# Transposing the decays of a linear attention without a clamp, and storing the first FFN's sums from another queue

## The chip, the cores and the metric

The kernel runs on one core of a Trainium2 chip. The metric is the device time of one execution in microseconds (us). A core has five engines with instruction streams of their own: PE (matrix products and transposes), DVE (vector), ACT (activations), POOL (GpSimd) and SP, which here only issues transfers. An engine runs its own instructions in order and waits on semaphores for the others. Transfers are issued from a queue of an engine, here SP's and, before the change, ACT's.

## The reference

A linear attention with decays is followed by two feed-forward networks (FFN) over the same 3072 tokens. There are B = 4 batches, H = 8 heads, S = 768 tokens and D = 48 features of a head:

```python
for t in range(S):
    cur = einsum('bhd,bhe->bhde', u[None] * k[t], v[t])
    y[t] = einsum('bhd,bhde->bhe', r[t], state + cur)
    state = w[t][..., None] * state + einsum('bhd,bhe->bhde', k[t], v[t])
x = y, as 3072 tokens of 384
h = x @ w_in;  x = (h * clip(h + 3, 0, 6) / 6) @ w_out             # 384 -> 2048 -> 384
h = x @ w_in2; s = h * softmax(h); x = (layernorm(s) * g) @ w_out2 # 384 -> 1024 -> 384
```

The decays w are drawn between 0.80 and 0.95. Everything is float32.

## The kernel before

The attention runs in chunks of 128 tokens. A tile is one chunk of one batch: 24 tiles, tile i being chunk g = i // 4 of batch b = i % 4. Four tiles make a group of 512 tokens, the width of a matrix product in the first FFN. Each tile passes five stages. `stw` checks that the decays lie in the range of the fast path (two activations on ACT that write `junk` and add up what lies outside) and clamps them; a kernel whose checks fire takes a general path. `st0` transposes w and r (`wt`, `rt`) and runs prefix products of the decays on DVE (`q` backwards, `e` forwards). `st1` transposes k and multiplies it into q, while POOL forms r * k * u (written over r) whose sums are `d`. `st2` makes `ktp`/`ktok`, the keys with tokens on the partitions, and the scores (`pa`), whose diagonal `am` POOL builds from d and DVE overwrites below the diagonal. `st3` adds the chunk to the state (`s_st`, over `sp`, the decayed state from POOL) and forms the output `yt`, which ACT and DVE split into a high part `xh` and a low part `xl`.

For tiles 0 to 9 the clamp writes a copy `wc`, which PE transposes: on DVE for tiles 0 to 3, on POOL for tiles 4 to 9. The tiles from 10 on (`LATE`) hold w, r and k in another layout (`late_w`, `late_r`, `late_k`), clamp `late_w` in place on POOL, and DVE transposes them (`flip`).

The first FFN runs in 96 slots n, 16 for each group of 512 tokens. `ffn_in(n)` is nine matmuls of 128x512 into a PSUM sum `h` (two buffers), ACT makes `t`, DVE finishes it, ACT rounds it to `gh`, and POOL or DVE forms the rest `gl`. `ffn_out` follows two slots later with nine matmuls into the three sums `y`. At the last of a group's 16, ACT scales the three sums into `ye` (L751) and its queue stores them to DRAM as `y1d` (L752). `ye` and `xl` rotate through the same two buffers. The weights of the first FFN come as packed words: during the first 16 slots SP loads a piece (`raw`, three buffers), and ACT and DVE decode it (`dec`, L50, L53, L66, then `w_h` on ACT and `w_l`, L72, on DVE).

Phase 2 is the second FFN over 24 tiles of 128 tokens, each read back from `y1d` by `load_y`. It starts after the 96 slots and the two that follow.

The order: for the first four tiles SP and POOL run in the order of the code; after that SP does, and DVE too from slot 78 (`NA`) on. All other engines are ordered by a scheduler when the program is built, which can therefore move any of their instructions when one is taken out. In a slot the loads of a late tile (`load_late`, the last of them `vt`) stand ahead of `ffn_out`, and so ahead of the stores.

Of the kernel before, what the change touches and what calls it, by code (L numbers as in the profile page):

```python
# [8 lines left out]
F32 = mybir.dt.float32  # L9
# [4 lines left out]
ALU = mybir.AluOpType  # L14
# [4 lines left out]
P = 128  # L19
W_LO, W_HI = 0.75, 1.25  # L20
# [258 lines left out]
def fast_path(  # L279
# [14 lines left out]
    nc = tc.nc  # L294
    B, H, S, D = r.shape
# [12 lines left out]
    NSLOT = NG * M1  # L308
# [7 lines left out]
    y1d = dram.tile([NG, P, KD, GT], F32, name="y1d")  # L316
# [25 lines left out]
        out=causal.bitcast(F32), in_=ones, pattern=[[1, P]], compare_op=ALU.is_gt, fill=0.0, base=0,  # L342
# [5 lines left out]
    atp = right.enter_context(tc.tile_pool(name="atp", bufs=2, side="right"))  # L348
# [28 lines left out]
    def w1_b(m):  # L377
        split(nc, dec_b(nc, *wst.pop(m)), w1_h[:, m, :], w1_l[:, m, :], nc.vector)
# [81 lines left out]
    def flip(nm):  # L460

        t = ps_tile(nm + "t")
        nc.vector.transpose(
            out=t.rearrange("p h (b j) -> p h j b", j=4),
            in_=late[nm].rearrange("p h (j d) -> p h j d", d=D)[:, :, :, 0:32],
        )
        return t
# [13 lines left out]
    def ps_in(i, nm, spare):  # L481
        if i >= B:
            return ps_tile(nm)
        return ps_y.tile([P, GT], F32, tag=spare, name=nm).rearrange("p (h t) -> p h t", t=P)

    def trans(dst, src):
        s2 = src.rearrange("p h d -> p (h d)")
        for hp in range(HP):
            nc.tensor.transpose(out=dst[0:DP, hp, :], in_=s2[:, hp * P:hp * P + DP], identity=ident)

    def stw(i):
        a = at[i]
        if i >= LATE:
            x = late["w"][:, :, 0:4 * D - 16]
            junk = atp.tile([P, HP, 4 * D - 16], mybir.dt.uint8, tag="junk", name="junk", bufs=1)
            nc.scalar.activation(
                out=junk, in_=x, func=ACTF.Relu, scale=-1.0, bias=b_lo, accum_out=chk[:, 3 * i:3 * i + 1]
            )
            nc.scalar.activation(
                out=junk, in_=x, func=ACTF.Relu, bias=b_hi, accum_out=chk[:, 3 * i + 1:3 * i + 2]  # L500
            )
            nc.gpsimd.tensor_scalar(out=x, in0=x, scalar1=W_HI, scalar2=W_LO, op0=ALU.min, op1=ALU.max)
            return
        wc = atp.tile([P, H, 64], F32, tag="wc", name="wc", bufs=1)
        flat = slice(0, H * 64 - 16)
        eng = nc.vector if i < B else nc.gpsimd
        eng.tensor_scalar(
            out=wc.rearrange("p h d -> p (h d)")[:, flat], in0=a["w"].rearrange("p h d -> p (h d)")[:, flat],
            scalar1=W_HI, scalar2=W_LO, op0=ALU.min, op1=ALU.max,
        )  # L510
        a["wc"] = wc
        junk = atp.tile([P, H, D], BF16, tag="junk", name="junk", bufs=1)
        nc.scalar.activation(
            out=junk, in_=a["w"][:, :, 0:D], func=ACTF.Relu, scale=-1.0, bias=b_lo, accum_out=chk[:, 3 * i:3 * i + 1]
        )
        nc.scalar.activation(
            out=junk, in_=a["w"][:, :, 0:D], func=ACTF.Relu, bias=b_hi, accum_out=chk[:, 3 * i + 1:3 * i + 2]
        )

    def st0(i):  # L520
        a = at[i]
        g = i // B
        if i < LATE:
            wt = ps_in(i, "wt", "y0")
            trans(wt, a["wc"])
            rt = ps_in(i, "rt", "y1")
            trans(rt, a["r"])
        else:
            wt, rt = flip("w"), flip("r")
        q = atp.tile([P, HP, C + 1], F32, tag="q", name="q")  # L530
        e = atp.tile([P, HP, C], F32, tag="e", name="e")
        nc.gpsimd.memset(q[0:DP, :, C:C + 1], 1.0)
        for hp in range(HP):
            nc.vector.tensor_tensor_scan(
                out=q[0:DP, hp, 0:C][:, ::-1], data0=wt[0:DP, hp, :][:, ::-1], data1=ones[0:DP, :],
                initial=1.0, op0=ALU.mult, op1=ALU.mult,
            )
        nc.vector.reciprocal(out=e[0:DP, :, 0], in_=q[0:DP, :, 0])
        for hp in range(HP):
            nc.vector.tensor_tensor_scan(  # L540
                out=e[0:DP, hp, 1:C], data0=wt[0:DP, hp, 0:C - 1], data1=ones[0:DP, 0:C - 1],
                initial=e[0:DP, hp, 0:1], op0=ALU.mult, op1=ALU.mult,
            )
        nc.vector.tensor_tensor(out=e[0:DP], in0=rt[0:DP], in1=e[0:DP], op=ALU.mult)
        a.update(q=q, e=e)
# [152 lines left out]
    def st3(i):  # L698
# [3 lines left out]
        out_x(i)  # L702

    stages = [stw, st0, st1, st2, st3]


# [29 lines left out]
    def ffn_out(n):  # L736
        g, m = divmod(n, M1)
        if m == 0:
            y_ps[g] = [ps_y.tile([P, GT], F32, tag=f"y{c}", name=f"y{c}") for c in range(KD)]
        gh, gl, _ = g_t.pop(n)  # L740
        for c in range(KD):
            cs = slice((KD + c) * P, (KD + c + 1) * P)
            wh, wl = w1_h[:, m, cs], w1_l[:, m, cs]
            for j, (a, b) in enumerate([(wh, gh), (wh, gl), (wl, gh)]):
                nc.tensor.matmul(  # L745
                    out=y_ps[g][c], lhsT=a, rhs=b, start=(m == 0 and j == 0), stop=(m == M1 - 1 and j == 2)
                )
        if m == M1 - 1:
            ye = xp.tile([P, KD, GT], F32, tag="xl", name="ye")
            for c in range(KD):  # L750
                nc.scalar.activation(out=ye[:, c, :], in_=y_ps[g][c], func=ACTF.Copy, scale=1.0 / 6.0)  # L751
                nc.scalar.dma_start(out=y1d[g, :, c, :], in_=ye[:, c, :])  # L752
            del y_ps[g]

    def range_in(ws):
# [42 lines left out]
    def w2_load(j):  # L798
        if j < M2:
            src = w_in2[:, 2 * j * P:2 * (j + 1) * P].rearrange("(k p) f -> p k f", p=P)  # L800
        else:
            src = w_out2[(j - M2) * P:(j - M2 + 1) * P, :].unsqueeze(1)
        wst[j] = [load_dec(nc, w2["dec"], src, bufs=3)]
# [17 lines left out]
    def load_y(i):  # L821
        g, b = divmod(i, B)
        t = w2["y"].tile([P, KD, C], F32, tag="y1", name="y1")
        nc.sync.dma_start(out=t, in_=y1d[g, :, :, b * C:(b + 1) * C])
        yh = w2["y"].tile([P, KD, C], F32R, tag="yh", name="yh")
        yl = w2["y"].tile([P, KD, C], F32R, tag="yl", name="yl")
        nc.gpsimd.tensor_scalar(out=yh, in0=t, scalar1=1.0, scalar2=1.0, op0=ALU.mult, op1=ALU.mult)
        nc.gpsimd.tensor_tensor(out=yl, in0=t, in1=yh.bitcast(F32), op=ALU.subtract)
        yt[i] = (yh, yl)
# [4 lines left out]
    def load_to(n):  # L834
        while nxt[0] < min(n, LATE):
            load_in(nxt[0])
            load_v(nxt[0])
            nxt[0] += 1
# [43 lines left out]
    for n in range(NSLOT + LAG):  # L882
        if n < NSLOT:
            ffn_in(n)
        if n == 4 * (JOIN - B) - 2:
            ps_late()
        for i, s in sorted(sched.get(n, []), key=lambda x: (x[0] - 2 * (x[0] >= JOIN and x[1] == 3), x[1])):
            stages[s](i)
            if s == NS - 1 and JOIN <= i + 1 < NTILE:
                state_in(i + 1)  # L890
            if s == 3:
                load_to(i + 3)
            if s == (0 if i + 1 == LATE else 2) and LATE <= i + 1 < NTILE:
                load_late(i + 1)
        if n >= LAG:
            ffn_out(n - LAG)
        if n + LD < M1:
            w1_b(n + LD)
        if n + LD + 1 < M1:
            w1_a(n + LD + 1)  # L900
        if n + LD + 3 < M1:
            w1_load(n + LD + 3)
        if n == M1:
            dec_st.close()
            late_open()
        if n == M1 + 1:
            late_mask("diag", ident)
        if n == M1 + 2:
            late_mask("mask", causal)
        if n == NA:  # L910
            row = range_a()
            right.close()
            w2_open()
            for j in range(3):
                w2_load(j)
            order.close()
            order = ctx.enter_context(ExitStack())
            order.enter_context(tc.manual_schedule(engines={mybir.EngineType.SP, mybir.EngineType.DVE}))
        j = n - NA
        if 1 <= j <= 2 * M2:  # L920
            w2_b(j - 1)
            if j + 2 < 2 * M2:
                w2_load(j + 2)
        if NA < n < NSLOT:
            ffn_low(n)
        if 0 <= j < 2 * M2:
            w2_a(j)
    load_y(0)
    load_y(1)
    order.close()  # L930


# [110 lines left out]
```

## Time and profile before

| | before |
|---|---|
| median of 3 runs | 775.6 us (774.93 to 776.07) |
| the profiled execution's own time | 774.71 us |
| its span, first to last instruction | 772.6 us |
| busy: PE, DVE, ACT, POOL | 733.3, 535.1, 333.1, 266.3 us |
| mean granted clock of PE | 0.971 |

A row of the trace's timeline gives the start, the duration, the engine, the line, the operation, the tiles (output <- inputs), and in brackets how long the engine had been idle and what ended that. "SPq" and "ACTq" are the sequencers that issue transfers. Where several instructions of a kind follow each other, the row gives their number and joint time. "PE rt <- issue" means that PE's transposes of r started after idle time that the trace puts down to nothing else.

### The profile page before, as it was taken

How to read it: one execution, taken by the hardware profiler on the slowest of the kernel's cores; microseconds unless marked ns; L12 is line 12 of the kernel's file. 1: busy time of each engine (PE TensorE's matmuls, PEld its weight loads, DVE VectorE, ACT ScalarE, POOL GpSimd, SP SyncE). 2: the span in 40 equal slices, each digit the busy share in tenths (PEclk: the TensorE clock that was granted, in tenths of full speed). 3: DMA queues.
4: the chain of work that ended last, by engine and by line, in shares of the span. 5: the costliest groups of instructions: out<-in, count | busy, mean ns of one | idle time of the engine just before them, and what ended most of it. 6: DMA issues, size and time to landing. Idle time of an engine off the chain costs nothing. (4 is left out here: it accounts for less than half of the span.)

```text
span 772.6 us, 14109 instructions
## 1 busy us (share of the span) xinstructions
PE 733.3 (95%) x5308; PEld 620.9 (80%) x5308; DVE 535.1 (69%) x1012; ACT 333.1 (43%) x647; POOL 266.3 (34%) x397
## 2 busy tenths in 40 slices
PE   5778797999999999999999999999999999999996
PEld 4556685888887888878888888888899999999995
DVE  6979889658777777777787865787555555555552
ACT  3455456334434333433334334654444444444442
POOL 5556547742332333333333311224322222222200
PEclk9669998999999999999999999999999999999998
DMA  9794754534344344443335203422111111111001
GB/s 168 172 172 124 178 133 101 108 86 97 86 95 121 86 104 87 93 117 82 91 74 130 63 1 103 144 94 70 65 48 44 41 42 48 45 42 42 31 22 36
DMA packets 151405, 67.31 MB, mean 87 GB/s; under 512 B 101792, under 2 KB 145952, under 8 KB 151328
## 3 DMA queue, kind: packets, MB, share of 16 engines
q1 hardware_dynamic: 148736, 61.60, 33.6%
q10 hardware_dynamic: 2592, 4.72, 1.6%
q8 instruction: 44, 0.72, 0.4%
q14 instruction: 33, 0.27, 0.1%
HBM read 56.33 MB, written 9.44 MB: 85 GB/s over the span
## 5 line engine op out<-in xcount | busy, mean ns | idle before, releaser
L745 PE MATMUL y<-gh,w_h 128*128 128x512 f32 x288 | 115.8, 402 | 0.0
L720 PE MATMUL h<-xh,w_h 128*128 128x512 f32 x288 | 113.4, 394 | 0.0
L720 PE MATMUL h<-xl,w_h 128*128 128x512 f32 x288 | 113.1, 393 | 0.0
L745 PE MATMUL y<-gl,w_h 128*128 128x512 f32 x288 | 113.1, 393 | 0.0
L745 PE MATMUL y<-gh,w_l 128*128 128x512 f32 x288 | 113.0, 392 | 0.0
L720 PE MATMUL h<-xh,w_l 128*128 128x512 f32 x288 | 112.7, 391 | 0.0
L726 ACT ACTIVATE gh<-t 128x512 fp32r<-128x512 f32 x96 | 60.4, 629 | 116.4 <-DVE t L725 116.4
L724 ACT ACTIVATE t<-h,cols 128x512 f32<-128x512 f32 x96 | 65.2, 680 | 93.2 <-PE h L720 91.2
L725 DVE SCALAR_TENSOR_TENSOR t<-t,h 128x512 f32<-128x512 f32 x96 | 65.1, 678 | 34.6 <-ACT t L724 34.3
L734 DVE TENSOR_TENSOR gl<-t,gh 128x512 fp32r<-128x512 f32 x80 | 66.7, 834 | 24.1 <-ACT gh L726 19.1
L78 DVE TENSOR_REDUCE nm<-h 128x1 f32<-128x1024 f32 x24 | 29.4, 1225 | 61.5 <-PE h L950 61.4
L977 PE MATMUL po<-w_oh,qh 128*128 128x384 f32 x192 | 67.2, 350 | 0.3 <-ACT qh L966 0.3
L745 PEld LDWEIGHTS y<-gh,w_h 128*128 128x128 f32 x288 | 54.3, 189 | 13.9 <-issue 3.2
L977 PE MATMUL po<-w_oh,ql 128*128 128x384 f32 x192 | 64.8, 337 | 0.1
L977 PE MATMUL po<-w_ol,qh 128*128 128x384 f32 x192 | 64.8, 338 | 0.0
L745 PEld LDWEIGHTS y<-gh,w_l 128*128 128x128 f32 x288 | 54.5, 189 | 11.8
L720 PEld LDWEIGHTS h<-xh,w_h 128*128 128x128 f32 x288 | 54.6, 190 | 11.5
L720 PEld LDWEIGHTS h<-xh,w_l 128*128 128x128 f32 x288 | 54.6, 190 | 11.4
L720 PEld LDWEIGHTS h<-xl,w_h 128*128 128x128 f32 x288 | 54.6, 190 | 11.3
L745 PEld LDWEIGHTS y<-gl,w_h 128*128 128x128 f32 x288 | 54.6, 190 | 10.4
L966 ACT ACTIVATE qh<-pt 128x512 fp32r<-128x512 f32 x48 | 26.1, 595 | 78.4 <-PE pt L964 78.4
L950 PE MATMUL h<-w_ih,yl 128*128 128x512 f32 x144 | 56.4, 392 | 0.0
(132 smaller groups left out, 1482.6 us busy)
## 6 DMA issues: line engine op xcount, KB each, us to landing
raw<-in_moe_w_out_dram SPq DMA_DIRECT2D x24, 384.0 KB, 6.2
raw<-in_moe_w_in_dram SPq DMA_DIRECT2D x48, 128.0 KB
r<-in_r_dram SPq DMA_DIRECT2D x24, 192.0 KB, 3.0
k<-in_k_dram SPq DMA_DIRECT2D x24, 192.0 KB, 4.2
y1d<-ye ACTq DMA_DIRECT2D x18, 256.0 KB, 3.2
y<-y1d SPq DMA_DIRECT2D x24, 192.0 KB, 2.7
out_dram<-os SPq DMA_DIRECT2D x24, 192.0 KB, 1.9
v<-in_v_dram SPq DMA_DIRECT2D x20, 192.0 KB, 4.7
```

Source lines behind the costliest of these rows:

```text
L78: nc.vector.tensor_reduce(out=nm, in_=h, axis=AX.X, op=ALU.max, negate=True)
L720: nc.tensor.matmul(out=h, lhsT=a, rhs=b, start=(j == 0), stop=(j == len(ops) - 1))
L724: nc.scalar.activation(out=t, in_=h, func=ACTF.Relu, bias=three)
L725: nc.vector.scalar_tensor_tensor(out=t, in0=t, scalar=6.0, in1=h, op0=ALU.min, op1=ALU.mult)
L726: nc.scalar.activation(out=gh, in_=t, func=ACTF.Copy)
L734: eng.tensor_tensor(out=gl, in0=t, in1=gh.bitcast(F32), op=ALU.subtract)
L745: nc.tensor.matmul(out=y_ps[g][c], lhsT=a, rhs=b, start=(m == 0 and j == 0), stop=(m == M1 - 1 and j == 2))
L950: nc.tensor.matmul(out=h[:, fs], lhsT=a[:, c, :], rhs=b_[:, c, fs], start=(j == 0), stop=(j == len(ops) - 1))
L966: nc.scalar.activation(out=qh[:, ms, :], in_=pt, func=ACTF.Copy)
L977: nc.tensor.matmul(out=po, lhsT=x[:, m, :], rhs=y[:, m, :], start=(n == 0), stop=(n == 3 * M2 - 1))
```

## The change

Three things. The clamp is gone from both layouts, and PE transposes the loaded w itself; the two checks on ACT and the general path stay. The stores of `ye` are issued by SP. The first two `load_y` stand in slot 94, ahead of the last group's stores, and no longer after the loop.

```diff
@@ stw
-            nc.gpsimd.tensor_scalar(out=x, in0=x, scalar1=W_HI, scalar2=W_LO, op0=ALU.min, op1=ALU.max)
             return
-        wc = atp.tile([P, H, 64], F32, tag="wc", name="wc", bufs=1)
-        flat = slice(0, H * 64 - 16)
-        eng = nc.vector if i < B else nc.gpsimd
-        eng.tensor_scalar(
-            out=wc.rearrange("p h d -> p (h d)")[:, flat], in0=a["w"].rearrange("p h d -> p (h d)")[:, flat],
-            scalar1=W_HI, scalar2=W_LO, op0=ALU.min, op1=ALU.max,
-        )
-        a["wc"] = wc
@@ st0
-            trans(wt, a["wc"])
+            trans(wt, a["w"])
@@ ffn_out
                 nc.scalar.activation(out=ye[:, c, :], in_=y_ps[g][c], func=ACTF.Copy, scale=1.0 / 6.0)
-                nc.scalar.dma_start(out=y1d[g, :, c, :], in_=ye[:, c, :])
+                nc.sync.dma_start(out=y1d[g, :, c, :], in_=ye[:, c, :])
@@ main loop
+        if n == NSLOT - 2:
+            load_y(0)
+            load_y(1)
         if NA < n < NSLOT:
             ffn_low(n)
         if 0 <= j < 2 * M2:
             w2_a(j)
-    load_y(0)
-    load_y(1)
```

The line numbers of the changed kernel are eight or nine lower from here on. What the change does to the order is seen at three places. The first is POOL around tile 3's diagonals (`am`) and tile 4's clamp. Before:

```order
L399 MEMSET w 128x8x16
L507 TENSOR_SCALAR wc<-w 128x496
L532 MEMSET q 112x4
L399 MEMSET r 128x8x16
L399 MEMSET k 128x8x16
L627 TENSOR_TENSOR am<-ident,d 128x512 x2
L399 MEMSET w 128x8x16
L507 TENSOR_SCALAR wc<-w 128x496
```

Now, the same stretch of POOL:

```order
L399 MEMSET w 128x8x16
L523 MEMSET q 112x4
L399 MEMSET r 128x8x16
L399 MEMSET k 128x8x16
L618 TENSOR_TENSOR am<-ident,d 128x512 x2
L399 MEMSET w 128x8x16
L551 TENSOR_TENSOR r<-r,k 128x8x48
```

No instruction that reads a loaded tile stands ahead of `am` any more. On ACT, too, the rounding `w_h` of weight piece 1 now stands ahead of the first check of tile 4, behind which it stood before.

The second is DVE at the end of tile 6 (its state sums, `s_st_117`) and the start of tile 7 (q from `wt`, later q times `kt`). Before:

```order
L53 SCALAR_TENSOR_TENSOR dec<-raw,dec 128x768
L649 TENSOR_TENSOR s_st_117<-kv,sp 48x4x48 x2
L66 TENSOR_SCALAR raw<-raw 128x768
L72 TENSOR_TENSOR w_l<-dec,w_h 128x768
L725 SCALAR_TENSOR_TENSOR t<-t,h 128x512
L691 TENSOR_TENSOR xl<-yt,xh 128x3x128
...
L544 TENSOR_TENSOR e<-rt,e 112x512
L725 SCALAR_TENSOR_TENSOR t<-t,h 128x512
L72 TENSOR_TENSOR w_l<-dec,w_h 128x768
L558 TENSOR_TENSOR q<-kt,q 112x4x128
```

Now:

```order
L53 SCALAR_TENSOR_TENSOR dec<-raw,dec 128x768
L716 SCALAR_TENSOR_TENSOR t<-t,h 128x512
L66 TENSOR_SCALAR raw<-raw 128x768
L72 TENSOR_TENSOR w_l<-dec,w_h 128x768
L640 TENSOR_TENSOR s_st_117<-kv,sp 48x4x48 x2
L682 TENSOR_TENSOR xl<-yt,xh 128x3x128
...
L535 TENSOR_TENSOR e<-rt,e 112x512
L716 SCALAR_TENSOR_TENSOR t<-t,h 128x512
L549 TENSOR_TENSOR q<-kt,q 112x4x128
L72 TENSOR_TENSOR w_l<-dec,w_h 128x768
```

The state sums moved behind t, L66 and w_l; the product q with `kt` moved ahead of w_l. On PE the transposes `rt` of tile 7 stand eight matmuls later than before.

The third is ACT at the end of the second group. Before:

```order
L751 ACTIVATE ye<-y_1882 128x512
L752 DMA y1d<-ye 128x512
L726 ACTIVATE gh<-t 128x512
L751 ACTIVATE ye<-y_1883 128x512
L751 ACTIVATE ye<-y_1884 128x512
L752 DMA y1d<-ye 128x512 x2
L724 ACTIVATE t<-h,cols 128x512
L589 ACTIVATE ktok<-ktp 128x448
```

Now:

```order
L742 ACTIVATE ye<-y_1862 128x512
L742 ACTIVATE ye<-y_1863 128x512
L717 ACTIVATE gh<-t 128x512
L742 ACTIVATE ye<-y_1864 128x512
L715 ACTIVATE t<-h,cols 128x512
L580 ACTIVATE ktok<-ktp 128x448
```

No store stands between the activations. On SP the three stores now stand in one piece behind the three `vt` loads, and ahead of the next tile's loads of `late_w`.

## Rows read from the trace of the kernel before

**Rows 1.** Windows: us, busy us of each engine (instructions), PEclk, DMA share, GB/s.
```profile
0.00:140.00 140.00, 109.73 (x889) 86.96 (x890) 119.33 (x210) 68.16 (x144) 80.80 (x109) 0.85 0.69 149
140.00:760.00 620.00, 617.90 (x4391) 529.14 (x4390) 414.47 (x801) 262.81 (x499) 185.45 (x288) 1.00 0.29 74
```

**Rows 2.** What PE waited for, whole span: us in total, times, longest us.
```profile
PE rt L489 <- issue: 7.6, 3, 4.6
PE ktp L587 <- DVE q L558: 5.5, 3, 4.1
...
PE yt L669 <- DVE am L630: 5.1, 2, 3.8
...
PE yt L662 <- ACT ktok L589: 2.0, 2, 1.1
```

**Rows 3.** The clamps' lines L507, L502: duration ns min/median/max, first and last start.
```profile
L507 POOL TENSOR_SCALAR wc<-w x6: 600/828/1191, 42.2 to 148.0; 128x496 f32<-128x496 f32 x6
L507 DVE TENSOR_SCALAR wc<-w x4: 479/604/1205, 4.1 to 24.5; 128x496 f32<-128x496 f32 x4
L502 POOL TENSOR_SCALAR late_w<-late_w x14: 773/775/777, 154.1 to 427.3; 128x704 f32<-128x704 f32 x14
```

**Rows 4.** Timeline around tile 3's diagonals and tile 4's clamp.
```profile
40.16 0.53 DVE L599 TENSOR_REDUCE d<-r 128x8 f32<-128x384 f32 x1
...
42.24 0.60 POOL L507 TENSOR_SCALAR wc<-w 128x496 f32<-128x496 f32 x1 [3.74 <-DMA w<-in_w_dram]
...
43.24 2.76 POOL L627 TENSOR_TENSOR am<-ident,d 128x512 f32<-128x512 f32 x2
...
43.66 1.44 DVE L72 TENSOR_TENSOR w_l<-dec,w_h 128x768 fp32r<-128x768 f32 x1 [2.09 <-ACT w_h L71]
```

**Rows 5.** Timeline: tile 4's d, the load behind it, and weight piece 6.
```profile
52.27 0.55 DVE L599 TENSOR_REDUCE d<-r 128x8 f32<-128x384 f32 x1 [1.37 <-POOL r L561]
...
53.00 3.29 SPq L400 DMA_DIRECT2D r<-in_r_dram  x1
...
68.56 0.91 ACT L63 ACTIVATE dec<-raw 128x768 f32<-128x768 f32 x1 [2.03 <-DMA raw<-in_moe_w_out_dram]
```

**Rows 6.** Timeline of DVE and PE at the end of tile 6 and in tile 7.
```profile
117.59 0.71 DVE L649 TENSOR_TENSOR s_st<-kv,sp 48x192 f32<-48x192 f32 x2
...
118.41 0.62 PE L489 MATMUL rt<-ident,r 128*112 128x128 f32 x4 [1.29 <-issue]
...
119.10 0.39 PE L745 MATMUL y<-gl,w_h 128*128 128x512 f32 x1
...
119.33 0.39 PE L745 MATMUL y<-gh,w_l 128*128 128x512 f32 x1
...
128.55 0.67 DVE L725 SCALAR_TENSOR_TENSOR t<-t,h 128x512 f32<-128x512 f32 x1
...
131.06 0.68 DVE L558 TENSOR_TENSOR q<-kt,q 112x512 f32<-112x512 f32 x1
```

**Rows 7.** Timeline: a subtract of POOL and a decoding step of DVE beside it.
```profile
88.88 1.99 POOL L734 TENSOR_TENSOR gl<-t,gh 128x512 fp32r<-128x512 f32 x1 [4.28 <-ACT gh L726]
...
89.66 2.03 DVE L53 SCALAR_TENSOR_TENSOR dec<-raw,dec 128x768 int32<-128x768 int32 x1
```

**Rows 8.** Timeline at the end of the second group: ACT's queue, SP and DVE.
```profile
248.47 1.03 ACTq L752 DMA_DIRECT2D y1d<-ye  x2
249.54 0.69 ACT L724 ACTIVATE t<-h,cols 128x512 f32<-128x512 f32 x1 [0.62 <-ACT ye L751]
...
252.38 1.67 SPq L437 DMA_DIRECT2D vt<-in_v_dram  x3
...
255.70 0.54 DVE L691 TENSOR_TENSOR xl<-yt,xh 128x384 fp32r<-128x384 f32 x1
```

**Rows 9.** The page's DMA issues: queue, count, KB each, median us to landing.
```profile
y1d<-ye ACTq DMA_DIRECT2D x18, 256.0 KB, 3.2
```

**Rows 10.** Timeline: the longest hold of DVE in one instruction after 140 us.
```profile
391.97 4.70 DVE L734 TENSOR_TENSOR gl<-t,gh 128x512 fp32r<-128x512 f32 x1 [0.30 <-ACT gh L726]
```

## The prediction

> **What bounds it now.** I read the windows first, then the waits of PE, then the timeline around each wait. The windows cut the run in two [rows 1]. From 140 to 760 us PE is busy 617.90 of 620 us, so nothing but fewer idle microseconds on PE can shorten that stretch, and there are about 2.1 of them. From 0 to 140 us PE is busy only 109.73 us, which leaves 30.3 us idle, while DVE is busy 119.33 of the 140. So in the front DVE, and what DVE waits for, sets the pace; PE waits behind it. The waits say the same by name [rows 2]: the long ones in the front end on DVE work (q, am), or on "issue" in front of rt, which is a place in PSUM that DVE gives back late. The 2.0 us on ktok, an ACT result, are the two gaps after 140 us. A saving counts if it shortens the front's DVE chain or removes one of those two gaps; anywhere else PE has other matmuls to run.
>
> **The clamps that go.** Four run on DVE (0.60, 0.48, 0.60, 1.21: 2.9 us), six on POOL for tiles 4 to 9 (0.60 to 1.19), fourteen on POOL for the late tiles (0.775 each) [rows 3]. The late fourteen are worth nothing: the view of that line lists nobody who waited for one of them, since the transpose behind each comes much later in DVE's order. I cost them at 0.
>
> **The four on DVE and the first one on POOL.** Taking 2.9 us out of DVE is not yet 2.9 us off the end: by hand through the new order I get about 1 us earlier at the scans of tile 2, 1.9 us after the 1.21 us clamp of tile 3, and then almost nothing, since the second and third pieces of the FFN weights were waited for as transfers there. What is left decides at 42 to 46 us [rows 4]. The clamp of tile 4 waited 3.74 us on POOL for the transfer of w, and the two diagonals of tile 3 (am) stood behind it, although their input d, started at 40.16, had been ready at 40.7. PE waited 3.8 us for that am [rows 2]. With the clamp gone POOL has nothing between: am can start at about 40.5 instead of 43.24. On ACT the rounding w_h of weight piece 1 now stands ahead of the range check of tile 4, which waits for the same transfer, so w_l need not wait its 2.09 us. The two together bring am, xl and the d of tile 4 forward by about 3.2 us (bounds: 2.1, the wait of w_l alone, to 3.8, the wait of PE).
>
> **What of that lasts.** Tile 4's d now ends 3.2 us earlier, and the r load of tile 6, which reuses the buffer that d reads, was issued right after it [rows 5]. But weight piece 6 is only issued behind tile 6's loads on SP, and ACT waited 2.03 us for it to land; DVE's own first step on that piece stands in its order just behind. The queue was slow there: one r load took 3.29 us to issue. If these transfers do not move, the whole 3.2 is given back at 69 us; if they move with d, it all stays. I take half, **-1.6** (bounds 0 and -3.2), because the load behind d moves, while the transfers ahead of it do not.
>
> **Tiles 6 and 7.** Before, the two state sums of tile 6 (s_st) ran at 117.59, right behind L53, and rt of tile 7 could then start, having waited 1.29 us [rows 6]. Now t, L66 and w_l stand ahead of s_st: 0.6 + 0.5 + 0.9, and 0.2 for gaps, is 2.2 us later. In exchange rt stands eight 512-column matmuls later on PE; at the 0.23 us from one start to the next [rows 6] that is 1.8 us of cover. Cost: **+0.4** (bounds 0 and +2.2). In tile 7 the product q*kt now stands ahead of w_l. Before it ran at 131.06 behind a w_l that waited for ACT; it can now follow t, which started at 128.55 and takes 0.6 to the next start, so at 129.15: **-1.9** out of the 4.1 us that PE waited for ktp [rows 2, 6] (bounds 0 and -1.9).
>
> **POOL out of DVE's way.** L53 took 2.03 us while POOL ran a subtract of 1.99 us from 88.88 [rows 7]; the DVE clamp that took 1.21 instead of 0.60 ran beside POOL work too. Six POOL clamps less could give DVE some of this back; I take 0 (bounds 0 and -1.0), since POOL moves its next subtract into the hole. The Trainium skill ("SBUF — State Buffer", section "SBUF: two separate sides") says that DVE and GpSimd share a pair of ports as an exclusive lock, held for a whole instruction, and that a DVE instruction with two SBUF inputs fully blocks against a GpSimd one that reads SBUF. The two rows agree with it: 2.03 is what L53 needs alone plus the rest of POOL's 1.99. By that rule each POOL clamp removed beside such an instruction would be a gain, and the sum would be lower by up to 1.0.
>
> **The stores moved to SP.** At the boundary of the second group ACT's queue gave 1.03 us to two stores, t came 0.62 us after the last ye, ktok after t, and PE waited 1.1 us for ktok [rows 2, 8]. Without stores ACT saves those 1.03 and the 0.3 of the first store, more than the 1.1. The third group has the same picture with 0.9: that is the 2.0 in two times of [rows 2]. I leave 0.2 for each: **-1.6** in all (bounds -2.0 and +2). On SP the three stores stand behind the vt loads of the same slot. Those were issued at 252.38 and took 1.67 us, so the stores go out from 254.1 and not from 247 to 249.5; with about 1 us for three issues and the 3.2 us to landing, which the page has for these stores [rows 9], the last lands near 258.3. The first xl of the next but one group takes that buffer, and it ran at 255.70: DVE may stand there for 2.6 us. I cost that at 0, because at 391.97 DVE was held for 4.70 us in one instruction [rows 10] in a stretch in which PE did not stop [rows 1]; without that cover it is 2.6 for each boundary. The Trainium skill ("DMA: Bandwidth & Descriptors", section "Issuing engines are not separate DMA queues") says that another issuing engine saves only the sequencer's time to start a transfer, usually small. Here that time is the 1.03 above, and by itself it would give about the same sum.
>
> **The first phase 2 loads.** PE goes from the last FFN matmul to the first of phase 2 without waiting on them, so their earlier place is worth 0. What hides them are the matmuls of the last slots, 18 a slot; without that cover a load would cost its issue and landing once, some 3 us, and the new place, ahead of three stores, is on the safe side of that.
>
> **Sum.** -1.6 + 0.4 - 1.9 + 0 - 1.6 = -4.7, say 770.0 against the profiled execution's own 774.7 (a span of 772.6 and 2.1 around it). The median of the runs, 775.6, lies 0.9 above that execution, so I forecast 770.9 against the median.
>
> **Rivals.**
> *More stays.* The transfers move with DVE: -3.2 at 46 us lasts, POOL's -1.0 is had, rt costs 0, the boundaries give 2.0: -8.1, or 767.5. For it: DVE has idle time enough in the front, 20.7 us of 140 [rows 1]. Against it: the 2.03 us wait for piece 6 [rows 5].
> *The front gives nothing.* Landings take back the 3.2, and PE's ktp waits for something else that is late, such as kt or the rounding on ACT: only the boundaries are left, -1.6, or 774.0. For it: in the front each engine waits in turn for the others, and POOL or ACT can be late next.
> *Slower: the stores hold xl.* At the four boundaries from the second to the fifth group DVE stands 2.6 us at xl, and behind it stand t of the running FFN slot and the scans. PE has two sums h in flight, and stops when both wait for t. If nothing covers it, this is +10.4, with -3.1 in the front and no gain at the boundaries: +7.3, or 782.9; with only half uncovered +2.1, or 777.7. It decides from the point where a hold of DVE is longer than PE's matmuls in hand; the 4.70 us hold speaks against it, but that one was in gl, not ahead of t.
> *It does not do what it says.* The stores on SP cost nothing, but ktok is still late for another reason (the three ye on ACT remain): the front alone, -3.1, or 772.5. It lies inside the range.
>
> **Chances.** Forecast 0.50, more stays 0.15, front gives nothing 0.17, ktok still late 0.07, slower 0.11. The range has to leave out the slower case and the far end of "more": from 766.5 to 775.5. A difference of 0.2%, 1.55 us, is about what a measurement of this kernel can tell from no change. Faster than 774.05: the forecast, more, ktok, and half of the nothing case, some of the forecast's mass lost to sizes I misjudge: 0.77. Within 0.2%: 0.12. Slower: 0.11.
>
> **What would show it.** Right: am of tile 3 starts before 41 us and PE's wait for am shrinks from 5.1 to about 1.5; tile 4's d starts near 49; ktp waits 2 to 3 us less; the ktok line is gone from PE's waits; PE is busy about 110 us in a front that ends 3 us earlier. Wrong: w_l or L50 of piece 6 waits longer on the raw transfer than the 2.03 on ACT (front gives nothing); rt of tile 7 waits over 3 us; xl waits on the y1d store with PE idle right behind (slower). The forecast also falls if PE's clock, 0.85 on average before 140 us [rows 1], a mean over stretches at either of its levels, falls further or less after the shorter stalls than it did.

## The result, and the profile after

The changed kernel takes 769.01 us in the median (767.82 to 770.91), the kernel before 775.7: a ratio of 0.9917, 95% interval 0.9904 to 0.9931. A second measurement, beside later runs, gave 768.86 and 0.9920 (0.9903 to 0.9937). The forecast was 770.9, within 766.5 to 775.5. The profiled execution took 769.93 us with a span of 768.2; that is 4.8 less than the profiled one of before, while the medians are 6.7 apart, since this one lies 0.9 above its median and that of before lay 1.0 below its own.

The windows of the changed kernel, which answer to [rows 1]:

```profile
0.00:140.00 140.00, 113.39 (x905) 87.80 (x906) 119.09 (x207) 68.32 (x145) 75.87 (x104) 0.88 0.69 149
140.00:760.00 620.00, 619.40 (x4397) 530.31 (x4397) 416.40 (x803) 263.75 (x501) 174.99 (x273) 1.00 0.30 75
```

PE is busy 3.7 us more in the first 140 us, and idle only 0.6 us in the 620 that follow. DVE is as busy in the front as it was (119.09 to 119.33): what it was spared in clamps it now does of later work. What PE waited for, as in [rows 2]:

```profile
PE rt L489 <- issue: 8.5, 3, 4.1
PE yt L660 <- DVE am L621: 7.8, 6, 2.8
PE wt L489 <- DMA w<-in_w_dram: 4.3, 1, 4.3
PE h L711 <- DVE w_l L72: 2.0, 1, 2.0
PE ktp L578 <- DVE q L549: 1.1, 2, 0.9
```

The ktok line is gone, ktp fell from 5.5 to 1.1; rt rose from 7.6 to 8.5 and am from 5.1 to 7.8. The profile of the second measurement has rt at 9.1 and am at 6.0.

One cut helps to read all the runs. The first `ye` of the first group marks the end of the front, the first `ye` of the last group the end of the five groups with boundaries between, and the rest is the last stores and phase 2. The marks are starts of ACT's rows in the timeline of one profiled execution of each kernel; the medians and ratios are those of the timed runs, each against the kernel before on the same chip.

| kernel | median us | ratio to before (95%) | first ye | to the last group's | rest |
|---|---|---|---|---|---|
| before | 775.7 | 1 | 162.65 | 379.85 | 230.10 |
| changed | 769.01 | 0.9917 (0.9904-0.9931) | 160.11 | 377.75 | 230.34 |
| changed, second measurement | 768.86 | 0.9920 (0.9903-0.9937) | 158.59 | 377.67 | 230.34 |
| before, stores on SP | 780.95 | 1.0076 (1.0059-1.0092) | 164.09 | 377.71 | 239.10 |
| before, loads moved | 775.17 | 1.0008 (0.9994-1.0021) | 164.01 | 379.92 | 230.07 |
| before, clamps out | 771.20 | 0.9959 (0.9943-0.9974) | 159.85 | 379.95 | 230.00 |
| changed, stores back on ACT | 771.88 | 0.9961 (0.9947-0.9976) | 159.18 | 379.87 | 230.05 |
| changed, loads back | 776.86 | 1.0018 (1.0006-1.0031) | 160.46 | 377.73 | 237.21 |
| changed, DVE's clamps back | 771.31 | 0.9953 (0.9934-0.9971) | 161.51 | 377.75 | 230.14 |
| changed, POOL's early clamps back | 771.20 | 0.9947 (0.9928-0.9966) | 161.70 | 377.84 | 230.26 |
| changed, late clamps back | 771.03 | 0.9953 (0.9934-0.9971) | 159.79 | 377.70 | 231.71 |
| changed, state sums first | 770.05 | 0.9939 (0.9925-0.9954) | 159.59 | 378.16 | 230.15 |
| changed, four w_l on POOL | 769.46 | 0.9940 (0.9923-0.9958) | 163.33 | 378.30 | 229.97 |
| changed, three buffers for q | 770.16 | 0.9933 (0.9917-0.9949) | 160.82 | 378.11 | 230.07 |

The middle column is the cleanest: 379.9 with the stores on ACT, 377.7 to 378.3 with them on SP, whatever else the kernel does. Between kernels that differ in the stores alone the move is worth 2.1 to 2.2 us there. The front has a spread of its own: the changed kernel itself ended it at 160.11 and at 158.59. The three kernels with all clamps end it at 162.65, 164.01 and 164.09, the five profiles without any clamp and with nothing else in the front altered between 158.59 and 160.46. The means, 163.6 and 159.6, lie 3.9 apart. One timed execution of the kernel with three buffers for q took 1036.63 us at a mean granted clock of 0.657; it is in that kernel's median and not in its ratio.

### The profile page after: what moved, and what is told of

It reads as the page before. It is cut to its first block, busy times and chain, and to the rows that moved or that the text cites. A ratio compares the mean times of both kernels' runs of the same rounds, so it can differ in the third digit from the quotient of the medians.

```text
span 768.2 us, 14066 instructions
## 1 busy us (share of the span) xinstructions
PE 734.3 (96%) x5308; PEld 619.3 (81%) x5308; DVE 535.5 (70%) x1008; ACT 332.6 (43%) x647; POOL 250.9 (33%) x377
## 5 line engine op out<-in xcount | busy, mean ns | idle before, releaser
L560 POOL TENSOR_TENSOR sp<-s_st,q 112x384 f32<-112x384 f32 x20 | 18.4, 920 | 162.9 <-PE yt L653 139.7
```

What stands on the lines that cost most here:

```text
L560: nc.gpsimd.tensor_tensor(out=sp[0:DP], in0=s_st[b][0:DP], in1=q[0:DP, :, 0:1].to_broadcast([DP, HP, 2 * D]), op=ALU.mult)
```

## Experiments: the parts one by one

**The stores alone.** The kernel before, with one word changed:

```diff
-                nc.scalar.dma_start(out=y1d[g, :, c, :], in_=ye[:, c, :])
+                nc.sync.dma_start(out=y1d[g, :, c, :], in_=ye[:, c, :])
```

> The kernel before with nothing changed but the queue of the 18 stores (SP, not ACT); PE's order is the one of before, row for row. My theory: the two gaps behind ktok (1.10 and 0.87 us in the profile of before) are the stores' doing and independent of the front, so the time is 775.7 - 2.0 = 773.7 us, the ktok line is gone from PE's waits, and the front's waits stay as they were (rt 7.6, ktp 5.5, am 5.1 us). Rival: the gaps vanished only because the front shifted the work around them; then the time stays at 775.7 and the gaps stand. Second rival (xl held by stores that land later on SP): PE waits new after 140 us, time 776 or more.

Measured: 780.95 us, slower by 6.5, although the ktok line is gone and the middle is 2.1 shorter. None of the three expectations had that: the second rival has the time, 776 or more, but not the cause, since in this trace no xl waited for a store. The loss is in the last column, 239.10 for 230.10. SP at the end of the FFN, first in the kernel before and then here:

```profile
524.30 5.81 SPq L824 DMA_DIRECT2D y<-y1d  x3
```

```profile
542.42 1.68 SPq L752 DMA_DIRECT2D y1d<-ye  x3
544.14 12.03 SPq L824 DMA_DIRECT2D y<-y1d  x5
547.08 0.51 POOL L827 TENSOR_SCALAR yh<-y 128x384 fp32r<-128x384 f32 x1 [9.49 <-DMA y<-y1d]
547.64 0.80 PE L950 MATMUL h<-w_ih,yh 128*128 128x512 f32 x1 [4.53 <-POOL yh L827]
```

Before, the first `y` loads went out at 524.3, some 18 us ahead of the last `ye`. Here they stand behind the last three stores on SP, which wait for those `ye`; so they go out at 544.14, and POOL's split and PE's first phase 2 matmul come after. Of the 9.0 us by which the column grew, 2.0 lie behind the last activation, 8.4 us from there to the end and not 6.3. The changed kernel with the late clamps back, whose loads are not behind the stores, has such a long end too (7.9). The 7.0 that are left agree with the next run.

**The loads put back.** The changed kernel without its third part:

```diff
-        if n == NSLOT - 2:
-            load_y(0)
-            load_y(1)
...
+    load_y(0)
+    load_y(1)
     order.close()
```

> The changed kernel with the first two loads of phase 2 again behind the loop, so behind the last three stores in SP's order. The kernel before with the stores alone moved to SP had 4.5 us of PE waiting for the first phase 2 tile and came out 6.5 us slower than before. My theory: that is this place; the time is 8 us above the changed kernel, about 777, with PE waiting 4 to 5 us for yh at the start of phase 2 and a lower clock behind it. Rival: the 6.5 us came from the front or from the boundaries; then the time stays at the changed kernel's.

Measured: 776.86, 8.0 above the changed kernel on the same chip, as expected. PE at the start of phase 2 of this kernel:

```profile
543.40 0.51 POOL L818 TENSOR_SCALAR yh<-y 128x384 fp32r<-128x384 f32 x1 [9.41 <-DMA y<-y1d]
...
543.96 0.80 PE L941 MATMUL h<-w_ih,yh 128*128 128x512 f32 x1 [4.45 <-POOL yh L818]
...
546.06 0.63 PE L941 MATMUL h<-w_il,yh 128*128 128x512 f32 x1
546.49 0.63 PE L941 MATMUL h<-w_ih,yl 128*128 128x512 f32 x1
...
549.08 0.39 PE L941 MATMUL h<-w_ih,yh 128*128 128x512 f32 x1
549.30 0.40 PE L941 MATMUL h<-w_il,yh 128*128 128x512 f32 x1
```

and the window in between, which gives the granted clock (the last figure but two):

```profile
546.00:548.00 2.00, 2.00 (x6) 1.55 (x5) 0.00 (x0) 0.00 (x0) 0.55 (x1) 0.50 0.35 103
```

The wait is 4.45 us. Behind it the matmuls start 0.43 us apart (546.06, 546.49) and later 0.22 to 0.23: after the idle stretch PE first ran at the lower of its clock's two levels, at 0.50, and from 549 on at 1.00. The first ten matmuls take 4.65 us (543.96 to 548.61) where ten later ones take 2.3, which is another 2.4 us. That makes 6.8 of the 6.9 by which the last column grew. The rest of the 8.0 between the medians is not in that column; in this execution the front was 1.9 longer too (160.46 for 158.59).

**The loads alone.** In the kernel before, the same three lines moved into slot 94, stores on ACT.

> The kernel before with the first two phase 2 loads moved ahead of the last stores and nothing else. The same move was worth 8.0 us where SP has the stores. With the stores on ACT's queue my theory gives it 0: those loads were issued well before the end of the FFN in the kernel before too; 775.0, within 1 us, and no wait of PE at the start of phase 2 either way. Rival: the move is worth something by itself, 773 or less.

Measured: 775.17, ratio 1.0008 (0.9994 to 1.0021): nothing, and no wait at the start of phase 2. So the third part has no worth of its own. The second part needs it: with it the stores' move is a gain of 2.2 in the middle column, without it the whole is a loss of 6.5.

**The stores put back on ACT**, in the changed kernel.

> The changed kernel with the 18 stores back on ACT's queue; PE's order is the one of the changed kernel, row for row. My theory: the boundaries cost 2.0 us again, so 769.0 + 2.0 = 771.0 us, with about 2 us of PE waiting for ktok, and the front as in the changed kernel. Rival: with the front earlier the gaps don't come back, 769.0 us.

Measured: 771.88, a ratio of 0.9961 beside the changed kernel's 0.9920, so about 3 us lost; the waits for ktok are back with 2.0 us in two times. By the middle column it is 2.1. The rest lies within what the front varies from one execution to another.

**The clamps alone.** The kernel before without clamps, everything else as it was.

> The kernel before with the clamps taken out and nothing else: stores on ACT, first phase 2 loads behind the loop. The whole change took 6.2 us off; of these the two boundary gaps are 2.0, so my theory gives the clamps alone 4.2 us: 775.0 - 4.2 = 770.8, or 0.9946 of before, with 2.0 us of PE waiting for ktok as before. The run with the stores alone back on ACT's queue (0.9961) should agree with it. Rival: the clamps' gain is only had together with the stores' move; then 773 or more.

Measured: 771.20, ratio 0.9959 (0.9943 to 0.9974), with ktok's 2.0 us still there. It agrees with the run above, so the clamps' going gives 3 to 4 us and needs nothing from the other parts.

## Experiments: where the front's gain sits

**DVE's clamps back, POOL's clamps back.** In the changed kernel, the copy `wc` again for tiles 0 to 3 on DVE, or for tiles 4 to 9 on POOL:

```diff
+        a["wc"] = a["w"]
+        if i < B:                      # the other run: i >= B, on nc.gpsimd
+            wc = atp.tile([P, H, 64], F32, tag="wc", name="wc", bufs=1)
+            nc.vector.tensor_scalar(out=wc[...], in0=a["w"][...], scalar1=W_HI, scalar2=W_LO, ...)
+            a["wc"] = wc
...
-            trans(wt, a["w"])
+            trans(wt, a["wc"])
```

> The changed kernel with the clamp of tiles 0 to 3 back on DVE, and no other clamp. My theory: the front's gain, 2.6 us in the profile, comes from the 2.9 us that DVE is spared, so the time is 2 to 3 us above the changed kernel's and ktp of tile 2 is 2 us later than there. Rival: it comes from POOL's clamps of tiles 4 to 9; then the time stays within 1 us of the changed kernel's.

> The changed kernel with the clamp of tiles 4 to 9 back on POOL, and no other clamp. My theory (DVE's clamps are the gain): time within 1 us of the changed kernel's, am of tile 3 again behind the clamp of tile 4 at about 43 us. Rival (POOL's clamps are the gain): 2 to 3 us above it. If both this and the run with DVE's clamps stand 2 us higher, the two gains don't add.

Measured: 771.31 and 771.20, both 2.4 above the changed kernel on that chip. Neither theory held alone. Their fronts end at 161.51 and 161.70, about halfway between the kernels with and without clamps, so by this column each half is worth about 2 us. The two losses add up to 4.8, more than the 3 to 4 that all the clamps cost, so their sizes are known to 1 us at best. The early transposes show DVE's half: ktp of tile 2 starts at 29.13 before, at 27.00 and 27.64 in the changed kernel's two profiles, at 30.14 with DVE's clamps back and at 27.56 with POOL's. POOL's half shows where the prediction looked for it, at am of tile 3. With POOL's clamps back:

```profile
41.65 0.60 POOL L507 TENSOR_SCALAR wc<-w 128x496 f32<-128x496 f32 x1 [1.48 <-DMA w<-in_w_dram]
...
42.62 2.04 POOL L627 TENSOR_TENSOR am<-ident,d 128x512 f32<-128x512 f32 x2
```

The memset of q ahead of that clamp had ended at 40.17; the clamp then held am until 42.62, which the changed kernel started at 40.71 in the profile of its second measurement.

**The late clamps back**, one line in the late layout, 14 instructions.

> The changed kernel with the 14 clamps of the late tiles back on POOL. My theory: nobody waits for them and POOL has room, so the time stays within 1 us of the changed kernel's 768.9, though 10.9 us of POOL work come back. Rival: DVE's transposes of late_w wait for POOL; then new waits of DVE there, PE idle after 150 us, and 1 to 3 us more.

Measured: 771.03, 2.2 above the changed kernel, which I had not expected; the two medians come from different chips, and by the ratios, 0.9953 to 0.9920, it is 2.6. The timeline does not put the difference on the clamps. They run between the first `ye` and the fifth group, and there this kernel takes 377.70 us, the changed one 377.67 and 377.75. Its front, 159.79, lies between the changed kernel's two, 158.59 and 160.11, with PE, DVE and ACT in the same order. What stands out is 1.4 us behind the last activation: 7.9 us from there to the end and not 6.5. The kernel before with the stores on SP had the same, 8.4; the other profiles have 6.2 to 6.6. What makes that end longer was not tried, and so neither theory is shown. A difference of 2 us between two kernels is thus no proof of a part, unless the timeline shows it at that part; for the two runs above it does so in the front, at ktp of tile 2 and at am of tile 3.

**State sums first.** In the changed kernel PE waited 8.5 us for a PSUM place in front of rt. The sums of tiles 4 to 9 with priority in DVE's order:

```diff
-                nc.vector.tensor_tensor(out=dst, in0=src, in1=a["sp"][o:o + D, :, f:f + D], op=ALU.add)
+                with tc.high_priority() if i < JOIN else ExitStack():
+                    nc.vector.tensor_tensor(out=dst, in0=src, in1=a["sp"][o:o + D, :, f:f + D], op=ALU.add)
```

> The changed kernel with the state sums s_st of tiles 4 to 9 given a higher priority in DVE's order (in tiles 5 and 6 they move ahead of two to four decoding steps). PE waited 0.6, 4.1 and 3.9 us for rt of tiles 5, 6 and 7 in the changed kernel. My theory: rt waits for the PSUM place that s_st gives back, so these 8.5 us fall below 3 us and the time falls by 2 to 5 us, to 764 to 767. Rival: DVE is the limit of the front, and the same microseconds come back in front of another matmul (the FFN's h behind w_l, am, ktp); then rt's waits fall but the time stays within 1 us of 769.0.

Measured: 770.05, ratio 0.9939 (0.9925 to 0.9954), no gain over the changed kernel, whose ratios are 0.9917 and 0.9920. Its waits of PE:

```profile
PE yt L661 <- DVE am L621: 8.2, 5, 3.1
PE ktp L578 <- DVE q L549: 5.3, 3, 2.6
...
PE h L712 <- DVE w_l L72: 1.8, 1, 1.8
PE kt L489 <- DVE xl L683: 1.6, 1, 1.6
...
PE rt L489 <- PE wt L489: 1.2, 2, 0.8
```

The wait for rt fell to 1.2 us as planned, which shows that rt had waited for the place that s_st gives back, and ktp, am and kt took it over, all of them behind DVE. In the first 140 us PE stood 27.4 us here and 26.6 in the changed kernel. So the rival has the mechanism: here the order of DVE's work decided at which matmul PE stood, not how long it stood in all. Its time, within 1 us of 769.0, is missed by a little; by the ratios this kernel is about 1.5 us slower than the changed one, with intervals that overlap.

**Work taken off DVE.** Four of the subtracts w_l moved to POOL:

```diff
-        split(nc, dec_b(nc, *wst.pop(m)), w1_h[:, m, :], w1_l[:, m, :], nc.vector)
+        split(nc, dec_b(nc, *wst.pop(m)), w1_h[:, m, :], w1_l[:, m, :], nc.gpsimd if m in (6, 9, 12, 15) else nc.vector)
```

> The changed kernel with the subtract w_l of weight pieces 6, 9, 12 and 15 on POOL and not on DVE. It tests whether DVE is the limit of the front that is left: DVE is spared 4 times 0.95 us, POOL gets 4 times about 2 us. My theory: 1 to 3 us less than the changed kernel's 768.9. Rival: POOL's am and gl come later and the port shared with DVE gives the rest back; then 769 or more, with PE's wait for am above the 6.0 us that it was.

Measured: 769.46, ratio 0.9940 (0.9923 to 0.9958): no gain, level with the changed kernel or a little above. PE's wait for am was 7.3 us in the profile, above the 6.0 that the rival names; but the changed kernel's other profile has 7.8, so this sign tells nothing. That execution took 773.37, far above its median, so I read no more from it. Whether fewer microseconds on DVE, without new ones on POOL, would shorten the front further stays open.

**A third buffer for q.** POOL's diagonals of tile 3 had stood behind a memset of q that waited for PE. Three buffers, `bufs=3`, in the tile of q:

> The changed kernel with three buffers for q and not two; DVE's order stays row for row. In the changed kernel POOL's am of tile 3 began at 42.4 us and not at 40.5 as forecast, behind a memset of q that had waited 6.9 us for PE's scores pa of tile 3. My theory: that memset is the new wait; with a third buffer am starts at about 40.6 and PE's wait of 1.6 us for it at 44.4 falls to under 0.3, so tile 4 starts about 1.3 us earlier; of the end 0 to 1.3 us are left, 767.7 to 769.0. Rival: am still starts at 42.4 because it waits for something else, and the time stays at 769.0.

Measured: 770.16, ratio 0.9933 (0.9917 to 0.9949). The edit did not do what it was for. POOL in this kernel:

```profile
42.63 0.10 POOL L523 MEMSET q<- 112x4 f32 x1 [6.91 <-PE pa L596]
...
42.97 2.04 POOL L618 TENSOR_TENSOR am<-ident,d 128x512 f32<-128x512 f32 x2
```

The scheduler used the third buffer to issue one memset earlier, and the next one, for a tile still later, took its place ahead of am with the same wait of 6.91 us. The time is level with the changed kernel or a little above. So the cause is seen, but that am would start at 40.6 without the memset was not shown.

## Why the prediction was right, and where its steps were not

The sum had -4.7 against the profiled execution, and the profile has -4.4 in span: the front 2.54 shorter (forecast 3.1), the middle 2.1 (1.6), the rest 0.24 longer (0). Over the profiles of the table the front's gain is nearer 3.9 and the middle's 2.2; these are 1.4 above the sum's terms, most of the 1.9 between 770.9 and 769.0. But within the front the sizes were wrong: more was gained by 112 us than I had, 4.2, and more given back in tile 7, so that the end of the front came out close by errors that offset each other, which is luck. The prediction's own signs say so too. Of those for being right, the ktok line is gone and ktp waits less, but in the first profile am of tile 3 began after 41 us, d of tile 4 at 51.4 and not near 49, and PE's wait for am rose to 7.8 instead of falling to 1.5. Of those for being wrong two were there: ACT waited 3.29 us for weight piece 6, and rt of tile 7 waited 3.88.

**The am of tile 3: the step failed.** I had it start at 40.5 once the clamp was gone. In the first profile it started at 42.40:

```profile
32.66 0.66 ACT L642 ACTIVATE s_st<-kv 48x192 f32<-48x192 f32 x2 [3.34 <-PE kv L631]
...
33.35 0.91 ACT L63 ACTIVATE dec<-raw 128x768 f32<-128x768 f32 x1
...
34.38 1.18 DVE L66 TENSOR_SCALAR raw<-raw 128x768 int32<-128x768 int32 x1 [1.41 <-ACT dec L63]
...
36.84 1.51 PE L660 MATMUL yt<-am,v 128*32 128x128 f32 x24 [2.81 <-DVE am L621]
...
39.22 2.77 PE L596 MATMUL pa<-e,q 48*128 48x128 f32 x16
...
39.95 0.54 DVE L590 TENSOR_REDUCE d<-r 128x8 f32<-128x384 f32 x1
...
42.05 0.11 POOL L523 MEMSET q<- 112x4 f32 x1 [6.91 <-PE pa L596]
...
42.40 2.05 POOL L618 TENSOR_TENSOR am<-ident,d 128x512 f32<-128x512 f32 x2
...
44.37 0.65 PE L660 MATMUL yt<-am,v 128*32 128x128 f32 x8 [1.57 <-DVE am L621]
...
51.36 0.55 DVE L590 TENSOR_REDUCE d<-r 128x8 f32<-128x384 f32 x1 [0.27 <-POOL r L552]
```

Two things. Between the clamp and am in POOL's order there was a memset of q, in the fence of orders ahead of the prediction too, and it waits until PE's scores `pa` of tile 3 have read q; they ended at 41.99. I had read only "no instruction that reads a loaded tile" and not asked what a memset waits for, though in the profile of before POOL had waited 13.4 us in four times there. And the scores themselves came later than before: ACT now had the state sums of tile 2 ahead of a decoding step, stood 3.34 us for PE's kv, and DVE's L66 and the am of tile 2 stood behind that. So d of tile 4 was 0.9 us earlier (51.36 to 52.27 of [rows 5]), not 3.2.

In the profile of the second measurement the order is the same, but ACT stood only 1.66 us for kv and PE's scores ended at 40.31:

```profile
40.37 0.10 POOL L523 MEMSET q<- 112x4 f32 x1 [4.59 <-PE pa L596]
...
40.71 2.04 POOL L618 TENSOR_TENSOR am<-ident,d 128x512 f32<-128x512 f32 x2
```

There am starts at 40.71 and d of tile 4 at 49.70, 2.6 us earlier than before. So the time that I forecast can come about, but not for my reason, that POOL has nothing between: in both executions am starts when PE's scores of its own tile have ended, and that moved by 1.7 us from one execution to the other.

**What lasted: more than half.** I took half of 3.2 because the landing of weight piece 6 would not move with DVE. ACT waited 3.29 us for it, not 2.03:

```profile
67.65 0.91 ACT L63 ACTIVATE dec<-raw 128x768 f32<-128x768 f32 x1 [3.29 <-DMA raw<-in_moe_w_out_dram]
```

The piece landed 0.9 us earlier than before [rows 5] while rt of tile 5 ran 3.4 us earlier (64.23 for 67.58). So the landing did hold ACT back, as I had it, but it gave back little of PE's lead. At ktp of tile 5 the kernel was 1.8 us ahead by the clock, and PE had five more of the FFN's matmuls behind it there (73 for 68, counted in the timelines), 1.1 us at 0.23 each: about 3 us lasted, not 1.6. How the lead had grown to that while d of tile 4 was only 0.9 earlier was not traced.

Tile 6 adds to it. PE's wait ahead of rt was 4.10 us and not 4.55, and behind it four matmuls ran 0.43 us or more apart and not ten. The granted clock (the last figure but two) in the windows behind that wait, first of before and then of the changed kernel:

```profile
94.00:99.50 5.50, 5.13 (x14) 4.20 (x15) 5.00 (x12) 1.18 (x4) 4.80 (x6) 0.50 0.49 154
```

```profile
92.00:95.00 3.00, 2.92 (x10) 2.52 (x11) 2.99 (x6) 1.02 (x2) 2.16 (x3) 0.54 0.69 201
```

The prediction had named the clock as something that could upset the forecast, and had no term for it; over the first 140 us the mean rose from 0.85 to 0.88.

**Tiles 6 and 7: the signs right, the sizes wrong.** The rows that answer to [rows 6]:

```profile
110.10 0.56 PE L631 MATMUL kv<-v,ktok 128*48 128x48 f32 x16
...
117.84 0.71 DVE L640 TENSOR_TENSOR s_st<-kv,sp 48x192 f32<-48x192 f32 x2
...
118.65 1.06 PE L489 MATMUL rt<-ident,r 128*112 128x128 f32 x4 [3.88 <-issue]
...
127.19 0.68 DVE L549 TENSOR_TENSOR q<-kt,q 112x512 f32<-112x512 f32 x1
127.92 0.60 PE L578 MATMUL ktp<-ident,q 112*128 112x112 f32 x4 [0.18 <-DVE q L549]
...
138.40 0.50 PE L711 MATMUL h<-xh,w_l 128*128 128x512 f32 x1 [1.99 <-DVE w_l L72]
```

rt of tile 7 waited 3.88 us, 2.6 more than before, beyond the bound of 2.2 that I had set to a cost of 0.4: PE had come to it 2.3 us earlier (114.77 for 117.12), and s_st ran no earlier than before (117.84 to 117.59) in spite of that. kv had ended at 110.66, so seven microseconds of DVE's order stood between. In return ktp waited 0.18 and not 4.10, a gain of 3.9 for the 1.9 of the forecast, and w_l, moved behind q*kt, cost 1.99 at 138.40, which I had not had. Net of the three: +2.6 - 3.9 + 2.0 = +0.7, where the sum had -1.5, so that the net has the other sign. What the front gained by 112 us, where wt of tile 7 started 4.2 earlier (112.27 for 116.47), it partly lost again there: wt of tile 8 started 2.5 earlier (143.87 for 146.41). The waits are 0.7 of these 1.7; in the rest PE was busy longer, and that was not traced. In the second profile rt waited 3.81 us and that w_l cost 0.77.

**POOL's room: right at 0.** DVE's four decoding lines took 17.9, 16.3, 16.1 and 11.8 us before; the groups of the changed kernel are

```profile
L50 DVE SCALAR_TENSOR_TENSOR dec<-dec,raw 128x768 int32<-128x768 int32 x16 | 17.7, 1104 | 0.0
L53 DVE SCALAR_TENSOR_TENSOR dec<-raw,dec 128x768 int32<-128x768 int32 x16 | 16.7, 1043 | 0.0
L72 DVE TENSOR_TENSOR w_l<-dec,w_h 128x768 fp32r<-128x768 f32 x16 | 16.3, 1016 | 2.9 <-ACT w_h L71 2.7
L66 DVE TENSOR_SCALAR raw<-raw 128x768 int32<-128x768 int32 x16 | 13.3, 830 | 3.2 <-ACT dec L63 3.2
```

64.0 together for 62.1. In the other profiles they take 61.1 and 62.3 us with all clamps and 62.5 to 63.7 without. Six instructions less on POOL did not make DVE's any shorter. At L53 one sees it: the step that took 2.03 us beside POOL's subtract [rows 7] took 2.04 here, with the same subtract beside it. (My reading of it was a little off: the rest of POOL's subtract was 1.21 us, and with the 0.94 of an undisturbed L53 that makes 2.15.) For the other steps the reason was not traced. So the gain of up to 1.0 that I had worked out beside the Trainium skill's rule on the shared ports ("SBUF — State Buffer", section "SBUF: two separate sides") was not had.

**The boundaries: mechanism right, size 0.5 low.** At the end of the second group:

```profile
245.75 0.70 ACT L715 ACTIVATE t<-h,cols 128x512 f32<-128x512 f32 x1
246.32 0.57 ACT L580 ACTIVATE ktok<-ktp 128x448 f32<-128x448 f32 x1
...
248.67 1.68 SPq L437 DMA_DIRECT2D vt<-in_v_dram  x3
...
250.45 1.52 SPq L743 DMA_DIRECT2D y1d<-ye  x3
...
254.25 0.69 DVE L716 SCALAR_TENSOR_TENSOR t<-t,h 128x512 f32<-128x512 f32 x1
254.86 0.55 DVE L682 TENSOR_TENSOR xl<-yt,xh 128x384 fp32r<-128x384 f32 x1
```

t and ktok follow ye without a store between, and PE has no gap: both gaps went in full, 2.0. The rival in which xl is held did not come about. The stores stand behind vt as forecast, but they were all issued by 251.97 and landed 2.4 us after issue (the page of the changed kernel; 3.2 in [rows 9]), ahead of xl at 254.86, which in the changed order stands behind a t that waited for PE anyway. Nobody waited for a `y1d` store in this trace.

**The first phase 2 loads at 0: right for the change, wrong as a reason.** I costed them against the kernel before, where the loads stood on a queue without the stores, and called the new place "on the safe side" of some 3 us. Each part has to be costed on top of the other: with the stores on SP the old place costs 8.0 by the medians. In the forecast this changes nothing, since the change makes both moves; but someone who had taken over only the stores from it would have been 6.5 us slower.

## What to carry to other kernels

When an instruction moves to a queue that runs in the order of the code, list what stands behind it there to the end of the stage, not only what stands ahead of it; the worst of it here was 20 us and a stage away. When something is taken out of an engine's order, read what the next instructions in that order wait for, memsets too, before taking the old wait as the gain. And where one engine is nearly full and the others wait for it in turn, bound a front by runs of parts, since its waits move from matmul to matmul and one execution differs from the next by 1 to 2 us.

## What was not expected of the hardware

How long a store takes to land differs as much between profiles with the same issuing queue as between the two queues. In the profiles of before and after, a store of 256 KB took 3.2 us when ACT's queue had issued it and 2.4 when SP's had, in all 18 (3.2/3.2/3.2 and 2.3/2.4/2.4, minimum, median, maximum), which looks like a property of the queue. But the medians of all fourteen profiles are 2.5, 2.8, 3.0 and 3.2 from ACT's queue and 2.3 to 2.7 from SP's, where single stores took up to 3.0: the two overlap, so these runs do not show that the queue makes the difference. The Trainium skill says that transfers issued by different engines run on the same DMA engines ("DMA: Bandwidth & Descriptors", section "Issuing engines are not separate DMA queues"); the overlap is in line with it.

Two profiles of one kernel, with PE, DVE and ACT in the same order, end the front 1.5 us apart (158.59 and 160.11), and the time behind the last activation was 6.2 to 6.6 us in twelve profiles and 7.9 and 8.4 in two. And an idle stretch of 4.45 us on PE cost about half as much again behind it, through ten matmuls at the lower clock.
